# Background transfers of a two-block attention kernel sent one by one from a list, and its output operands added later

## The chip, the cores and the metric

The kernel runs on one core of a Trainium2 chip. The metric is the device time of one execution in microseconds; before the change the median of 3 runs is 2736.03 us (2734.36 to 2736.89).

## The reference

Two attention blocks work on the same input x (2048 tokens x 512) with weights of their own, and a gate mixes their outputs. All is float32; each block has 32 heads of 16 elements.

```python
def block(x, wqkv, wo):
    q, k, v = split_heads(x @ wqkv)              # 32 heads, each 2048 x 16
    p = softmax(einsum("bhqd,bhkd->bhqk", q, k) * 16 ** -0.5, axis=-1)
    return merge_heads(einsum("bhqk,bhkd->bhqd", p, v)) @ wo

g = sigmoid((x * gate_w).sum(-1, keepdims=True))
out = g * block(x, A_wqkv, A_wo) + (1 - g) * block(x, B_wqkv, B_wo)
```

## The kernel before, in words

The two blocks make 64 heads, in 8 groups (G = 0 to 7) of 8; groups 0 to 3 are block A. A head takes 16 *rounds*, so there are 1024. The main loop (lines 889 to 927) does four rounds in one *pass*: it runs through the string FULL letter by letter, and each letter puts one piece of work into the engines' queues, in an order that was written by hand.

- `e` computes a bank of scores (PE, L257) and its exponential (ACT, L259); a pass has 16 of them. The stationary rows of a head are its *stacks* k_st, q_st and x_st, read from DRAM by `load_stacks` (12 DMAs on SP, one head after next). Two more rows of q_st hold minus the row maximum, so that the exponent is already safe.
- `m`, `D` and `A` compute these maxima 14 rounds ahead, from a second set of scores (PE L188; DVE L194 and L206; ACT L201). Half a head's maxima at a time, every 8 rounds, are split into two float16 parts on GpSimd (`max_split`, L217 to L220, buffer mrow), transposed on DVE, and sent by SP to a DRAM buffer md and from there into q_st (`max_rows`, L227 and L230). The next scores of that half need them about one pass later.
- digits multiply p by v on PE (L835, operand vg, loaded by GpSimd in `load_v`). Every 8 rounds the accumulator goes out through ev to DRAM (od, L859), numerators and denominators together.
- `W` advances the *stream* `hidden()` by one step: the projections q, k and v of later heads (L276, L298), and at last the output projection (L576). `E` evicts a finished bank of it. What `W` finds not ready stays empty.

The stream has two phases. In the first it needs weights: w (one for each of q and k of a group, 512 KB, `load_w`) and w_big (for v, then wo of either block, 2 MB, `load_rows`). In the second, after group 7's projections, it needs each group's attention output: `prepare` sets a job for one of 14 pairs (G, i): `load_num` (8 DMAs of 128 KB: ot and o_part from od), `load_rb` (4 DMAs of 128 KB, the inverted denominators rb), then on GpSimd `add_num` (12 rounds after the loads) and `normalize` (3 rounds later). `later` holds such calls by round, and `due` runs them in the middle of a pass or at its start. The denominators come in with `load_den`, and are added and inverted by `add_den` (GpSimd) and `queue_inverse` (DVE).

Almost all DMAs are issued on the SP queue, in program order. SP waits at each one whose data another engine has still to write (od waits for ev, md for DVE, rd and the parts of q and k for DVE and GpSimd), and all DMAs behind it wait too; one that needs nothing is issued as soon as SP reaches it. The DMAs of SP use eight completion semaphores in turn, so at most eight are in flight. GpSimd executes in order as well.

Before the loop `first_projections` makes q and k of group 0 (eight banks split into `early`, three buffers), v of group 0 follows in half banks (`store_half_v`, to vd), the first half of head 0's maxima is computed beside them (`run_ahead`), and vg is loaded.

Of the kernel before, what the change touches and what calls it, by code (L numbers as in the profile page):

```python
# [33 lines left out]
P = 128  # L34
# [20 lines left out]
def gated_mha(ctx: ExitStack, tc: tile.TileContext, xT, x, wqkv_a, wo_a, wqkv_b, wo_b, gate_w, out):  # L55
# [42 lines left out]

    wqk = {}

    def load_w(queue, G, isk, k=0, n=None):
# [4 lines left out]
        load_rows(queue, wqk[G, isk], wqkv[s][:, o:o + P], k, n or KH)  # L106

    for k in range(0, KH, 2):
# [30 lines left out]

    def load_stacks(h, queue=nc.sync):  # L140
        dma, dma_q = nc.sync.dma_start, queue.dma_start
        s, hh = divmod(h, H)
        g, j = divmod(hh, HG)
        q, k = q_st[h % 3], k_st[h % 3]
        qs, ks, xs = qd[s][g], kd[s][g], xd[s][g]

        def pairs(t, step, n=S):
            v = t[0, j]
            return bass.AP(tensor=v.tensor, offset=v.offset, ap=[[n, DH], [step, 2], [1, n]])

        for b in HALVES:
            dma(k[b:b + 32], pairs(ks, HG * DH * S))
            dma_q(q[b:b + 32], pairs(qs, 0))
            dma(k[b + 32:b + 48], ks[0, j])
            dma_q(q[b + 32:b + 48], qs[1, j])
        x = x_st[h % 2]
        for b in HALVES:
            dma(x[b:b + 32], pairs(xs, HG * DH * 512, 512))
            dma(x[b + 32:b + SC], xs[0, j])

# [202 lines left out]
    def first_projections():  # L363
        early, rise = {}, xs.tile([P, 512], F32, name="rise_k")

        def split(isk, i, side, ps):
            t = early[isk, i, side] = xs.tile([P, 2, 512], F16, name="early", bufs=3)
            act.activation(t[:, 0], ps, AF.Copy, scale=UNIT)
# [26 lines left out]
    first_projections()  # L395
    load_stacks(0, nc.scalar)
    new_maxima(0)
# [144 lines left out]
    def load_num(G, i):  # L542
        k = SLOTS[G, i]
        part = nums["p", G, i] = T["late"].tile([P, 2, 512], F32, name="o_part", bufs=2)
        o = od[G]
        for p in range(2):
            for f, b in enumerate((64, 0)):
                for hh in range(2):
                    nc.sync.dma_start(
                        T["o"][b:b + 64, k + hh] if p == 0 else part[b:b + 64, hh],  # L550
                        bass.AP(tensor=o.tensor,
                                offset=o.offset + ((4 * hh * 2 + i) * 4 + 2 * p + f) * 32 * 512,
                                ap=[[2 * NQ * 32 * 512, 4], [512, DH], [1, 512]]))
# [5 lines left out]
    def load_rb(G, i):  # L559
        rb = nums["r", G, i] = T["late"].tile([P, 2, 512], F32, name="rb", bufs=2)  # L560
        r = rd[G]
        for f, b in enumerate((64, 0)):
            for hh in range(2):
                nc.sync.dma_start(rb[b:b + 64, hh],
                                  bass.AP(tensor=r.tensor, offset=r.offset + 4 * hh * S + i * 1024 + f * 512,
                                          ap=[[S, 4], [0, DH], [1, 512]]))

# [96 lines left out]
    for G in range(LAST):  # L664
        end = (G + 1) * HG * NT
        at(end + 4, load_den, G)
        at(end + 7, add_den, G)
        for i in range(4):
            at(end + 8 + 2 * i, queue_inverse, G, i)
    end = LAST * HG * NT  # L670
    for i in range(2):
        at(end + 6 + 4 * i, load_num, 6, i)
        at(end + 18 + 4 * i, add_num, 6, i)
        at(end + 23 + 4 * i, load_rb, 6, i)
        at(end + 32 + 4 * i, normalize, 6, i)
    now = [0]

    def until(r):
# [34 lines left out]
    def soon():  # L713
        return now[0] // 4 * 4 + 8

    def hidden():
# [12 lines left out]
        def qk(G):  # L729
            for isk in (1, 0):  # L730
                if isk:
                    load_w(nc.sync, G, 0)
                elif G < LAST:
                    load_w(nc.sync, G + 1, 1)
                for low in (0, 64):
# [4 lines left out]
        for G in range(1, NG):  # L740
            yield from qk(G)
            if G == 1:
                for n in range(8):
# [24 lines left out]

        r = soon()
        for G in range(4):  # L770
            ready = prepare(G, 0, r + 8 * G)
        for G in range(2):
            prepare(G, 1, r + 32 + 8 * G)
        yield from until(ready)
        yield from outs(range(4), 0, first)
        r = soon()
        for G in (2, 3):
            ready = prepare(G, 1, r + 8 * (G - 2))
        for G in (4, 5):
            done_b = prepare(G, 1, r + 16 + 8 * (G - 4))  # L780
        yield from until(ready - 5)
        yield from outs(range(4), 1, first)
        for b in HALVES:
            nc.sync.dma_start(w_big[b:b + 64, :6], wo[1][:384].rearrange("(k p) c -> p k c", p=64))
        nc.sync.dma_start(w_big[:DH, 6], wo[1][DM - DH:, :])
        nc.sync.dma_start(w_big[DH:, 6], wo[1][DM - P:DM - DH, :])
        r = soon()
        for G in (4, 5):
            prepare(G, 0, r + 8 * (G - 4))
        yield from until(max(done_b, r + 4))  # L790
        yield from outs((4, 5), 1, more)
        yield from until(LAST * HG * NT + 36)
        yield from outs((4, 5, 6), 0, more)
        yield from outs((6,), 1, more)

    stream = hidden()

# [91 lines left out]
    while r < ROUNDS:  # L889
# [9 lines left out]
        for code in order:  # L899
            if code == "e":  # L900
                if scored == 8:
                    due(r + 2)
                    if (r + 2) % NT == 4 and r // NT + 2 < NH:
                        load_stacks(r // NT + 2)
                score(2 * r + scored // 2, scored % 2)
                scored += 1
            elif code in "mDA":
                step(code)
            elif code == "E":
                empty()  # L910
            elif code == "W":
                now[0] = r + scored // 4
                next(stream, None)
# [48 lines left out]
```

## Time and profile before

| | |
|---|---|
| median of 3 runs | 2736.03 us |
| the profiled execution | 2732.4 us |
| its span | 2730.5 us |
| PE busy | 2543.5 us, 93% |
| ACT busy | 2401.1 us, 88% |
| DVE busy | 2375.3 us, 87% |
| GpSimd (POOL) busy | 410.2 us, 15% |
| PE's mean granted clock | 0.977 |
| moved by SP's queue (q1) | 172.81 MB, 22.5% of 16 DMA engines' time |

In the page's lines a digit is the busy share of a slice of 1/40 of the span, 68 us. In the view of waits a row reads: engine, what it was about to do, whose end it waited for, then the total in us, how often, and the longest. SPq is SP's queue, where only issuing takes time.

### The profile page before, as it was taken

Reading aid. Unit: us, or ns where it says so; the run is one execution under the profiler, and the core shown is the slowest. Engines: PE = TensorE matmul, PEld = TensorE weight load, DVE = VectorE, ACT = ScalarE, POOL = GpSimd, SP = SyncE. Lnnn points to the kernel's source line nnn. Section 1 sums busy time; section 2 is a strip of 40 time slices with the busy share of each in tenths; the row PEclk is TensorE's granted clock in tenths of the full one; section 3 lists DMA queues with packets and bytes.
Section 4 is the critical chain, followed back from the end, with each engine's and each line's share of the span. In section 5 each row is a group of like instructions: output and inputs, shape, how many; then the busy total and the mean of one; then the engine's idle time right before and its main releaser. Section 6 shows DMA issues by size and latency. Waiting matters only on the chain.

```text
span 2730.5 us, 169615 instructions
## 1 busy us (share of the span) xinstructions
PE 2543.5 (93%) x76566; PEld 1611.9 (59%) x76566; DVE 2375.3 (87%) x4604; ACT 2401.1 (88%) x4741; POOL 410.2 (15%) x809
## 2 busy tenths in 40 slices
PE   8899999999999999999999998689987998979987
PEld 4566665666666666666666665346644655545553
DVE  2889998999999999999999998679986988978884
ACT  1589998999999999999999998679986988978885
POOL 2133112111100001111111110121011001010003
PEclk9899999999999999999999999889998999989999
DMA  7422223232222212232222213222122122121103
GB/s 156 115 72 74 79 75 87 64 83 62 55 58 67 75 53 62 66 86 62 60 59 76 76 55 92 94 93 59 41 87 75 50 71 85 45 75 46 38 21 111
DMA packets 143790, 195.07 MB, mean 71 GB/s; under 512 B 38600, under 2 KB 88728, under 8 KB 143064
## 3 DMA queue, kind: packets, MB, share of 16 engines
q1 hardware_dynamic: 137528, 172.81, 22.5%
q8 instruction: 599, 9.81, 1.5%
q0 software_dynamic: 2560, 8.91, 1.3%
q10 hardware_dynamic: 2976, 2.49, 0.4%
q14 instruction: 127, 1.04, 0.1%
HBM read 117.56 MB, written 66.58 MB: 67 GB/s over the span
## 4 chain that ended last, share of the span: by engine, by line
PE 71%; DVE 10%; DMA 8%; POOL 3%; ACT 3%; issue 3%; SPq 1%; ACTq 0%; POOLq 0%; DVEq 0%
PE acc L835 33%; PE ps_m L188 13%; PE ps_st L257 12%; DVE mxp L194 6%; PE ps_p L276 5%; DMA md<-mt 4%; PE ps_st L188 3%; PE ps_p L576 2%; ACT p L259 2%; DVE ev L858 1%; PE ps_p L298 1%; DVE rise L206 1%; DMA o_part<-od 1%; ACT ev L858 1%; POOL stage L725 1%
## 5 line engine op out<-in xcount | busy, mean ns | idle before, releaser
L259 ACT ACTIVATE p<-ps_st 128x512 f32<-128x512 f32 x4068 | 2122.3, 640 | 190.3 <-PE ps_st L257 140.2
L835 PE MATMUL acc<-p,vg 64*17 64x384 f32 (+1 forms) x34784 | 2207.9, 368 | 22.9 <-issue 6.5
L194 DVE TENSOR_REDUCE mxp<-ps_m 128x1 f32<-128x512 f32 x3072 | 1944.8, 682 | 184.8 <-PE ps_m L188 152.7
L257 PE MATMUL ps_st<-q_st,k_st 50*32 50x512 f16 x16272 | 1568.7, 384 | 95.3 <-DMA q_st<-md 83.9
L188 PE MATMUL ps_m<-k_st,q_st 48*32 48x512 f16 x14336 | 1393.1, 381 | 24.0 <-DVE mxp L194 19.8
L835 PEld LDWEIGHTS acc<-p,vg 64*17 64x17 f32 x34784 | 982.3, 94 | 252.1 <-issue 27.8
L257 PEld LDWEIGHTS <-k_st 50*32 50x32 f16 x16384 | 665.8, 91 | 462.6 <-issue 202.4
L188 PEld LDWEIGHTS <-q_st 48*32 48x32 f16 x16384 | 549.7, 91 | 269.7 <-issue 178.2
L276 PE MATMUL ps_p<-x_sb,w 64*32 64x512 f32 x3648 | 480.9, 593 | 2.3 <-issue 2.3
L206 DVE CUSTOM_DVE_ANT_0 rise<-ps_m,rise 128x512 f32<-128x512 f32 x512 | 349.6, 683 | 69.5 <-PE ps_st L257 54.0
L201 ACT ACTIVATE rise<-ps_st 128x512 f32<-128x512 f32 x512 | 314.9, 615 | 60.7 <-PE ps_st L188 52.9
L576 PE MATMUL ps_p<-w_big,ot 64*32 64x512 f32 x1792 | 236.9, 593 | 27.0 <-DVE o_acc L767 25.1
L188 PE MATMUL ps_st<-x_st,q_st 48*32 48x512 f16 x2048 | 225.5, 380 | 0.2 <-ACT v_st L341 0.2
L218 POOL TENSOR_SCALAR mrow<-mrow 128x8 f32<-128x8 f32 x128 | 29.6, 232 | 1209.0 <-DVE mrow L217 1208.4
L322 POOL CAST parts<-stage 128x512 f16<-128x512 f32 x56 | 34.1, 608 | 830.7 <-DVE stage L702 437.0
L276 PE MATMUL ps_p<-w_big,x_sb 64*32 64x512 f32 x1024 | 134.6, 590 | 0.0
L276 PEld LDWEIGHTS ps_p<-x_sb,w 64*32 64x32 f32 x3648 | 117.1, 107 | 17.9 <-issue 4.1
L298 PE MATMUL ps_p<-w_big,x_sb 64*32 64x256 f32 x1280 | 87.5, 377 | 0.6 <-issue 0.6
L576 PEld LDWEIGHTS ps_p<-w_big,ot 64*32 64x32 f32 x1792 | 56.0, 107 | 46.6 <-DVE o_acc L767 28.0
L323 POOL TENSOR_TENSOR parts<-stage,parts 128x512 f16<-128x512 f32 x56 | 65.2, 1164 | 4.6
L298 PEld LDWEIGHTS ps_p<-w_big,x_sb 64*32 64x32 f32 x1280 | 43.6, 106 | 14.2 <-issue 2.8
L858 DVE COPY ev<-acc 128x512 f32<-128x512 f32 x64 | 44.1, 690 | 0.5 <-PE ps_m L188 0.2
(107 smaller groups left out, 766.7 us busy)
## 6 DMA issues: line engine op xcount, KB each, us to landing
od<-ev SPq DMA_DIRECT2D x126, 256.0 KB
k_st<-kd SPq DMA_DIRECT2D x128, 128.0 KB
q_st<-qd SPq DMA_DIRECT2D x126, 128.0 KB
vd<-v_st SPq DMA_DIRECT2D x64, 136.0 KB
vg<-vd POOLq DMA_DIRECT2D x32, 272.0 KB, 3.7
k_st<-kd SPq DMA_DIRECT2D x128, 64.0 KB
q_st<-qd SPq DMA_DIRECT2D x126, 64.0 KB
kd<-parts SPq DMA_DIRECT2D x56, 128.0 KB
```

The costliest lines, as they stand in the source:

```text
L188: pe.matmul(ps[j:j + 32], q[b:b + SC, t * P + j:t * P + j + 32], k[b:b + SC], start=True, stop=True, tile_position=(b, j))
L194: dve.tensor_reduce(o[:, c:c + 1], ps, op=ALU.max, axis=AX.X)
L201: act.activation(rises[m], ps, AF.Relu)
L206: dve.tensor_tensor_reduce(out=rise, in0=ps, in1=rise, scale=1.0, scalar=LOWEST, op0=ALU.add, op1=ALU.max, accum_out=o[:, 0:1])
L257: pe.matmul(ps[j:j + 32], k[b:b + SC + 2, kk * P + j:kk * P + j + 32], qv(b), start=True, stop=True, tile_position=(b, j))
L259: act.activation(pt[u][:, c * 512:(c + 1) * 512], ps, AF.Exp, scale=SCALE / UNIT ** 2)
L276: pe.matmul(ps[j:j + 32], a, m, start=k == 0, stop=k == last, tile_position=(b, j))
L298: pe.matmul(ps[j:j + 32, e * 256:(e + 1) * 256], x_sb[b:b + 64, i, k, o:o + 32], w_big[b:b + 64, k, g * P:(g + 2) * P], start=k == e == 0, ...
L323: pool.tensor_tensor(t[:n, 1], v[:n], t[:n, 0], op=ALU.subtract)
L576: pe.matmul(ps[j:j + 32], T["o"][b:b + 64, k, o + j % 64:o + j % 64 + 32], w_big[b:b + 64, g], start=first, stop=last, tile_position=(b, j))
L835: pe.matmul(acc[d:d + 17, qa * P:qb * P], v[b:b + 64, 2 * (w % n) + c if h == NH - 1 else w % n, j], pt[u][b:b + 64, c * 512 + qa * P:c * ...
L858: (dve.tensor_copy if w < NT or h == NH - 2 else act.copy)(ev, acc)
```

## The change

There is a list `waiting` of single DMAs. `drip(n)` issues the first n of it. In the main loop it is called with 1 after every second score bank, so two DMAs go out in a round. Into the list go: the stacks (at the front, `waiting[0:0] = ops`), w in four DMAs of 128 KB instead of two of 256 KB, w_big in 16 of 128 KB instead of two of 1 MB (for block A's second half of v, eight of 128 KB), and the output operands, whose 12 DMAs of a job were single ones before. A `mark` in the list notes the round in which everything ahead of it is out.

The jobs are now set by a second stream, `prepared()`, advanced once in a round: it puts a job's loads into the list, waits for their mark, and sets `add_num` 6 rounds later and `normalize` 8 rounds later. `hidden()` waits for the round in which its operands are ready. `load_den` goes from round 4 to round 8 after a group's end, `add_den` from 7 to 13, the inversions from 8, 10, 12, 14 to 14 to 17. Before the loop `early` has five buffers instead of three, the first `max_rows` and the stacks of head 1 come two to four steps earlier (the stacks one by one), and the four loads of the first vg stand behind all of v instead of two and two between.

The core of the diff:

```diff
+    def drip(n):
+        for _ in range(n):
+            if waiting:
+                fn, *a = waiting.pop(0)
+                fn(*a)
...
+    def drip_rows(t, src, n, last=KH):
+        waiting.extend((part_rows, t, src, b, k, n) for k in range(0, last, n) for b in HALVES)
...
+        if slow:
+            waiting[0:0] = ops
...
-            t = early[isk, i, side] = xs.tile([P, 2, 512], F16, name="early", bufs=3)
+            t = early[isk, i, side] = xs.tile([P, 2, 512], F16, name="early", bufs=5)
...
-                elif gone == n_ahead // 2 + 3:
+                elif gone == n_ahead // 2 + 1:
                     max_rows(0, 0)
-                elif gone == n_ahead // 2 + 6:
+                elif gone == n_ahead // 2 + 2:
+                    drip_w(1, 1)
                     load_stacks(1)
-                    load_w(nc.sync, 1, 1)
+                elif gone > n_ahead // 2 + 3 and gone % 2:
+                    drip(1)
...
-        if t in (2, 6):
-            for c in (0, 2) if t == 2 else (1, 3):
-                load_v(0, c)
...
-    load_wv(0, 2, 2)
+    for c in (0, 1, 2, 3):
+        load_v(0, c)
+    drip_rows(w_big[:, :, 256:], wqkv[0][:, 2 * DM + 256:], 2)
+    waiting.append((mark, "v"))
...
-        at(end + 4, load_den, G)
-        at(end + 7, add_den, G)
+        at(end + 8, load_den, G)
+        at(end + 13, add_den, G)
...
-    def prepare(G, i, r):
-        r = max(r, (G + 1) * HG * NT + 22)
-        at(r, load_num, G, i)
-        at(r + 3, load_rb, G, i)
-        at(r + 12, add_num, G, i)
-        at(r + 15, normalize, G, i)
-        return r + 18
...
+    def prepared():
+        added = []
...
+            for G, i in jobs:
+                yield from until((G + 1) * HG * NT + 26)
+                while len(added) > 1 and now[0] < added[-2] + 3:
+                    yield
+                waiting.extend((fn,) for fn in (*load_num(G, i), *load_rb(G, i)))
+                waiting.append((mark, ("in", G, i)))
+                yield from wait(("in", G, i))
+                r = now[0] + 6
+                at(r, add_num, G, i)
+                at(r + 2, normalize, G, i)
+                added.append(r)
+                flags["ready", G, i] = r + 5
...
-                load_wv(1, 0, NG)
+                drip_rows(w_big, wqkv[1][:, 2 * DM:], 1)
...
-        load_rows(nc.sync, w_big, wo[0], 0, KH)
+        drip_rows(w_big, wo[0], 1)
...
+                if scored % 4 == 0:
+                    now[0] = r + scored // 4
+                    next(prep, None)
                 score(2 * r + scored // 2, scored % 2)
                 scored += 1
+                if scored % 2:
+                    drip(1)
```

Three places of the program show how the SP queue is changed. The first is the start of the second phase, on SP, around the maxima md_115 of head 41. Before (a row is a line of the kernel, the operation, out<-in, the shape, and how often in a row):

```order
L549 DMA ot<-od_105 64x1x512 x4
L549 DMA o_part<-od_105 64x1x512 x4
L859 DMA od_110<-ev 128x512
L564 DMA rb<-rd_116 64x1x512 x4
L227 DMA md_115<-mt 4x32x32
L230 DMA q_st_219<-md_115 2x1024 x2
L524 DMA rd_120<-rn 16x4x128 x2
L549 DMA ot<-od_106 64x1x512 x4
L549 DMA o_part<-od_106 64x1x512 x4
L859 DMA od_110<-ev 128x512
L564 DMA rb<-rd_117 64x1x512 x4
L227 DMA md_115<-mt 4x32x32
```

And after the change at the same place:

```order
L899 DMA od_110<-ev 128x512
L589 DMA ot<-od_105 64x1x512 x4
L262 DMA md_115<-mt 4x32x32
L265 DMA q_st_219<-md_115 2x1024 x2
L589 DMA o_part<-od_105 64x1x512 x4
L601 DMA rb<-rd_116 64x1x512 x4
L589 DMA ot<-od_106 64x1x512 x2
L899 DMA od_110<-ev 128x512
L561 DMA rd_120<-rn 16x4x128 x2
L589 DMA ot<-od_106 64x1x512 x2
L589 DMA o_part<-od_106 64x1x512 x2
L262 DMA md_115<-mt 4x32x32
```

Before each md stood twelve loads and an od; now four loads stand between the od (or rd) and md, and the rest of the job stands behind md.

The second place is on SP where block A's v is done and w_big is loaded with block B's weights, around md_115 of head 8. Before:

```order
L345 DMA vd_103<-v_st_230 64x2x272 x2
L97 DMA w_big<-in_wqkv_b 64x8x512 x2
L97 DMA w_11575<-in_wqkv_a 64x8x128 x2
L227 DMA md_115<-mt 4x32x32
L230 DMA q_st_219<-md_115 2x1024 x2
```

After, with the stacks of the next head (k_st_216 and the rows up to x_st_223) in front of what is left of the list:

```order
L380 DMA vd_103<-v_st_230 64x2x272 x2
L116 DMA w_big<-in_wqkv_b 64x512 x3
L262 DMA md_115<-mt 4x32x32
L265 DMA q_st_219<-md_115 2x1024 x2
L106 DMA k_st_216<-kd_88 32x1x2048
```

Ahead of md there were 2.5 MB; now there are three portions of 128 KB, and the other 13 of w_big follow 8 to 12 rounds later.

The third place is on SP before the loop, where the last rows of group 0's v go to vd. Before, the stacks of head 1 (12 DMAs, the last two shown) and w stood ahead of them:

```order
L158 DMA x_st_224<-xd_95 32x1x512
L159 DMA x_st_224<-xd_95 16x512
L97 DMA w_1324<-in_wqkv_a 64x8x128 x2
L345 DMA vd_103<-v_st_229 64x2x272 x2
L345 DMA vd_103<-v_st_230 64x2x272 x2
L97 DMA w_big<-in_wqkv_a 64x8x256 x2
L97 DMA w_1620<-in_wqkv_a 64x8x128 x2
```

After:

```order
L265 DMA q_st_211<-md_113 2x1024 x2
L106 DMA k_st_216<-kd_87 32x1x2048
L106 DMA q_st_215<-qd_79 32x1x2048
L106 DMA k_st_216<-kd_87 16x2048
L380 DMA vd_103<-v_st_229 64x2x272 x2
L380 DMA vd_103<-v_st_230 64x2x272 x2
L106 DMA q_st_215<-qd_79 16x2048
```

Three stack loads are left ahead of the vd stores; the rest of the stacks, w and w_big stand behind them.

More of the change, by code (lines that the diff above doesn't have):

```diff
@@ L99, in gated_mha @@
     wqk = {}
+    waiting = []
+    def drip(n):
[3 more added lines that the diff above has]
+                fn(*a)
     def load_w(queue, G, isk, k=0, n=None):
@@ L106, in load_w, with part_rows, drip_w, begin @@
         load_rows(queue, wqk[G, isk], wqkv[s][:, o:o + P], k, n or KH)
+    def part_rows(t, src, b, k, n):
+        nc.sync.dma_start(t[b:b + 64, k:k + n], src[k * 64:(k + n) * 64].rearrange("(k p) c -> p k c", p=64))
+    def drip_w(G, isk):
+        s, g = divmod(G, NG)
+        def begin():
+            wqk[G, isk] = xs.tile([P, KH, P], F32, name=f"w{isk}")
+        def one(b, k):
+            if (b, k) == (0, 0):
+                begin()
+            o = isk * DM + g * P
+            part_rows(wqk[G, isk], wqkv[s][:, o:o + P], b, k, 4)
+        waiting.extend((one, b, k) for b in HALVES for k in (0, 4))
+    def drip_rows(t, src, n, last=KH):
+        waiting.extend((part_rows, t, src, b, k, n) for k in range(0, last, n) for b in HALVES)
+    def mark(name):
+        flags[name] = now[0]
+    flags, now = {}, [0]
     for k in range(0, KH, 2):
@@ L138, in gated_mha, with load_stacks @@
         x_st.append(const.tile([P, 512], F16, name=f"x_st{i}"))
-    def load_stacks(h, queue=nc.sync):
+    def load_stacks(h, queue=nc.sync, slow=True):
         dma, dma_q = nc.sync.dma_start, queue.dma_start
@@ L149, in pairs @@
             return bass.AP(tensor=v.tensor, offset=v.offset, ap=[[n, DH], [step, 2], [1, n]])
+        x = x_st[h % 2]
+        ops = []
         for b in HALVES:
[L152 to L156, printed above, removed]
-        for b in HALVES:
-            dma(x[b:b + 32], pairs(xs, HG * DH * 512, 512))
-            dma(x[b + 32:b + SC], xs[0, j])
+            ops += [(dma, k[b:b + 32], pairs(ks, HG * DH * S)), (dma_q, q[b:b + 32], pairs(qs, 0)),
+                    (dma, k[b + 32:b + 48], ks[0, j]), (dma_q, q[b + 32:b + 48], qs[1, j])]
+        for b in HALVES:
+            ops += [(dma, x[b:b + 32], pairs(xs, HG * DH * 512, 512)), (dma, x[b + 32:b + SC], xs[0, j])]
+        if slow:
+            waiting[0:0] = ops
+        else:
+            for fn, *a in ops:
+                fn(*a)
     LOWEST = -3.4028234e38
@@ L395, in gated_mha @@
     first_projections()
-    load_stacks(0, nc.scalar)
+    load_stacks(0, nc.scalar, slow=False)
     new_maxima(0)
@@ L543, in load_num @@
         k = SLOTS[G, i]
-        part = nums["p", G, i] = T["late"].tile([P, 2, 512], F32, name="o_part", bufs=2)
         o = od[G]
@@ L548, in load_num, with one, load_rb @@
                 for hh in range(2):
[L549 to L553, printed above, removed]
+                    def one(p=p, f=f, b=b, hh=hh):
+                        if (p, f, hh) == (0, 0, 0):
+                            nums["p", G, i] = T["late"].tile([P, 2, 512], F32, name="o_part", bufs=2)
+                            nums["r", G, i] = T["late"].tile([P, 2, 512], F32, name="rb", bufs=2)
+                        nc.sync.dma_start(
+                            nums["p", G, i][b:b + 64, hh] if p else T["o"][b:b + 64, k + hh],
+                            bass.AP(tensor=o.tensor,
+                                    offset=o.offset + ((4 * hh * 2 + i) * 4 + 2 * p + f) * 32 * 512,
+                                    ap=[[2 * NQ * 32 * 512, 4], [512, DH], [1, 512]]))
+                    yield one
+    def load_rb(G, i):
+        r = rd[G]
+        for f, b in enumerate((64, 0)):
+            for hh in range(2):
+                def one(f=f, b=b, hh=hh):
+                    nc.sync.dma_start(nums["r", G, i][b:b + 64, hh],
+                                      bass.AP(tensor=r.tensor, offset=r.offset + 4 * hh * S + i * 1024 + f * 512,
+                                              ap=[[S, 4], [0, DH], [1, 512]]))
+                yield one
     def add_num(G, i):
@@ L557, in add_num @@
         pool.tensor_tensor(v, v, nums.pop(("p", G, i)), op=ALU.add)
[L559 to L566, printed above, removed]
     def normalize(G, i):
@@ L665, in gated_mha @@
         end = (G + 1) * HG * NT
-        at(end + 4, load_den, G)
-        at(end + 7, add_den, G)
+        at(end + 8, load_den, G)
+        at(end + 13, add_den, G)
         for i in range(4):
[L669 to L676, printed above, removed]
+            at(end + 14 + i, queue_inverse, G, i)
     def until(r):
@@ L703, in copier, with wait @@
             else dve.tensor_copy
-    def prepare(G, i, r):
-        r = max(r, (G + 1) * HG * NT + 22)
-        at(r, load_num, G, i)
-        at(r + 3, load_rb, G, i)
-        at(r + 12, add_num, G, i)
-        at(r + 15, normalize, G, i)
-        return r + 18
-    def soon():
-        return now[0] // 4 * 4 + 8
+    def wait(*names):
+        while any(n not in flags or flags[n] > now[0] for n in names):
+            yield
+    def prepared():
+        added = []
+        for name, jobs in (("phase", ((0, 0), (1, 0), (2, 0), (3, 0), (0, 1), (1, 1))),
+                           (("out", 0, 0), ((2, 1), (3, 1), (4, 1), (5, 1))),
+                           (("out", 0, 1), ((4, 0), (5, 0), (6, 0), (6, 1)))):
+            yield from wait(name)
+            for G, i in jobs:
+                yield from until((G + 1) * HG * NT + 26)
+                while len(added) > 1 and now[0] < added[-2] + 3:
+                    yield
+                waiting.extend((fn,) for fn in (*load_num(G, i), *load_rb(G, i)))
[6 more added lines that the diff above has]
+                flags["ready", G, i] = r + 5
     def hidden():
@@ L731, in qk @@
                 if isk:
-                    load_w(nc.sync, G, 0)
+                    drip_w(G, 0)
                 elif G < LAST:
-                    load_w(nc.sync, G + 1, 1)
+                    drip_w(G + 1, 1)
                 for low in (0, 64):
@@ L742, in hidden @@
             if G == 1:
+                yield from wait("v")
                 for n in range(8):
@@ L753, in hidden @@
         second_phase()
-        load_rows(nc.sync, w_big, wo[0], 0, KH)
+        flags["phase"] = now[0] + 2
         def outs(groups, i, evict):
@@ L767, in more @@
             dve.scalar_tensor_tensor(o, ps, gate[1][:, t:t + 1], o, op0=ALU.mult, op1=ALU.add)
[L769 to L774, printed above, removed]
-        yield from outs(range(4), 0, first)
[L776 to L781, printed above, removed]
-        yield from outs(range(4), 1, first)
[L783 to L790, printed above, removed]
+        yield from wait(*(("ready", G, 0) for G in range(4)))
+        yield from outs(range(4), 0, first)
+        flags["out", 0, 0] = now[0]
+        yield from wait(*(("ready", G, 1) for G in range(4)))
+        yield from outs(range(4), 1, first)
+        flags["out", 0, 1] = now[0]
+        drip_rows(w_big, wo[1], 1, 6)
+        waiting.append((nc.sync.dma_start, w_big[:DH, 6], wo[1][DM - DH:, :]))
+        waiting.append((nc.sync.dma_start, w_big[DH:, 6], wo[1][DM - P:DM - DH, :]))
+        waiting.append((mark, "wo"))
+        yield from wait("wo")
+        yield from until(now[0] + 4)
+        yield from wait(("ready", 4, 1), ("ready", 5, 1))
         yield from outs((4, 5), 1, more)
-        yield from until(LAST * HG * NT + 36)
+        yield from wait(*(("ready", G, 0) for G in (4, 5, 6)))
         yield from outs((4, 5, 6), 0, more)
+        yield from wait(("ready", 6, 1))
         yield from outs((6,), 1, more)
-    stream = hidden()
+    stream, prep = hidden(), prepared()
     end = ROUNDS - NT
@@ L911, in gated_mha @@
             elif code == "W":
-                now[0] = r + scored // 4
                 next(stream, None)
```

## The prediction

> **What bounds the kernel now.** The page first: how long, which engine, and where the busy digits dip.
>
> ```profile
> span 2730.5 us, 169615 instructions
> PE 2543.5 (93%) x76566; PEld 1611.9 (59%) x76566; DVE 2375.3 (87%) x4604; ACT 2401.1 (88%) x4741; POOL 410.2 (15%) x809
> PE   8899999999999999999999998689987998979987
> PEclk9899999999999999999999999889998999989999
> ```
>
> PE (TensorE) is at nine tenths nearly everywhere and dips at the start and in slices 25 to 37, so the 187 us in which it is idle lie in a few places. The view of waits names them; first PE's own, then two of ACT and POOL that matter at the start.
>
> ```profile
> PE ps_st L257 <- DMA q_st<-md: 83.9, 13, 14.0
> PE ps_p L576 <- DVE o_acc L767: 25.1, 21, 1.8
> PE ps_m L188 <- DVE mxp L194: 19.8, 26, 2.8
> PE ps_st L257 <- issue: 9.3, 2, 5.0
> PE acc L835 <- DMA vg<-vd: 5.9, 1, 5.9
> ACT early L368 <- DMA qd<-early: 10.6, 2, 6.7
> POOL vg L269 <- DMA vd<-v_st: 39.6, 2, 20.5
> ```
>
> One wait leads: 13 times PE stands before the score product of L257 because the row maxima of the head have not come back from DRAM (`max_rows`: mt to md, md to q_st). The first row below, from the page's list of DMAs, counts 128 such trips; only 13 made PE wait. What stands ahead of a late one on the SP queue is in the timeline of SP; the last three rows are a trip with nothing ahead of it.
>
> ```profile
> md<-mt SPq DMA_DIRECT2D x128, 8.0 KB
> ...
> 1715.95 2.27 SPq L549 DMA_DIRECT2D ot<-od  x4
> 1718.58 2.37 SPq L549 DMA_DIRECT2D o_part<-od  x4
> 1721.81 0.36 SPq L859 DMA_DIRECT2D od<-ev  x1
> 1722.22 3.55 SPq L564 DMA_DIRECT2D rb<-rd  x4
> 1726.81 0.54 SPq L227 DMA_DIRECT2D md<-mt  x1
> 1735.40 0.55 SPq L230 DMA_DIRECT2D q_st<-md  x2
> ...
> 1881.02 0.34 SPq L859 DMA_DIRECT2D od<-ev  x1
> 1886.14 0.58 SPq L227 DMA_DIRECT2D md<-mt  x1
> 1888.12 0.52 SPq L230 DMA_DIRECT2D q_st<-md  x2
> ```
>
> Alone, md is back after 1.98 us (1886.14 to 1888.12). Behind twelve operand loads it takes 8.6 us (1726.81 to 1735.40), though it moves only 8 KB. Two stretches show what the DMA engines do meanwhile (columns: busy of PE, PEld, DVE, ACT, POOL, then clock, DMA share, GB/s):
>
> ```profile
> 1727.00:1735.00 8.00, 8.00 (x244) 4.19 (x228) 7.81 (x16) 8.00 (x18) 2.02 (x1) 1.00 0.27 97
> 1672.00:1680.00 8.00, 6.37 (x182) 3.33 (x171) 7.26 (x14) 6.92 (x15) 0.00 (x0) 1.00 1.08 205
> ```
>
> While md hangs behind operand loads, a share of 0.27 of 16 engines is busy, so about four of them, at 97 GB/s: those loads run on a quarter of the engines, and md sits in the same quarter. A portion of 128 KB takes 131,072 / 97,000 = 1.35 us there. While w_big streams (second row), all engines are full at 205 GB/s, and PE is down to 6.37 of 8 us.
>
> Now what the dips cost. One pass of the hand-written order (4 rounds) has 16 score banks and so 16 ACTIVATEs of L259; counting these per stretch gives the pace and the excess (columns: us, ACT busy, clock, DMA share, GB/s).
>
> ```profile
> 600.00:1040.00 440.00, 383.84 (x739) 1.00 0.23 63
> 2341.00:2395.00 54.00, 49.93 (x96) 1.00 0.19 57
> 97.00:116.00 19.00, 8.34 (x16) 0.78 0.81 172
> 426.00:453.00 27.00, 17.50 (x33) 0.87 0.70 152
> 1675.00:1834.00 159.00, 100.31 (x193) 0.86 0.31 98
> 2003.00:2041.00 38.00, 25.45 (x50) 0.91 0.25 87
> 2041.00:2120.00 79.00, 50.81 (x97) 0.89 0.22 72
> 2216.00:2250.00 34.00, 25.24 (x49) 0.90 0.36 82
> 2395.00:2457.00 62.00, 41.87 (x80) 0.89 0.21 70
> ```
>
> Undisturbed the pace is 440 / 739 = 0.595 us a bank where a W step (a projection piece from the stream) fills in, 9.53 us a pass, and 54 / 96 = 0.5625 us, 9.00 us a pass, without W steps. The excess of the seven disturbed stretches: 19 - 16 x 0.595 = 9.5; 27 - 33 x 0.595 = 7.4; 159 - 193 x 0.5625 = 50.4; 38 - 50 x 0.5625 = 9.9; 79 - 97 x 0.595 = 21.3; 34 - 49 x 0.5625 = 6.4; 62 - 80 x 0.5625 = 17.0. The last six make 112.4 us. That is more than the 83.9 us of named waits because each wait also leaves a lower clock (0.86 to 0.91) and because the stretches with w_big (426, 1675, 2216) hold PE waits put down to "issue" instead.
>
> **The change part by part.** *Operand loads in portions.* In the second phase 14 jobs of twelve DMAs (ot, o_part, rb) stood in bursts of eight and four. Now they go out one at a time, two in a round, and the burst ahead of md is four portions at most. But SP is not paced by rounds: it runs ahead to its next gate (od, md or rd, which wait for another engine), so four portions between an od and the md behind it go out at once, about half a pass, 5 us, before md. Four take 4 x 1.35 = 5.4 us, so md meets an almost empty queue. Where portions before the od are still unfinished too, md meets up to four: I count six such trips in the new order. What a late trip costs is bounded by the pair above: 8.6 us instead of 1.98 is 6.6 us late, and PE waited
>
> ```profile
> 1737.12 0.40 PE L257 MATMUL ps_st<-q_st,k_st 50*32 50x512 f16 x4 [1.89 <-DMA q_st<-md]
> ```
>
> 1.89 us, so 4.7 us are covered by the distance between the trip and its first use. Four portions (5.4 us) cost up to 0.7 us, and with SP itself late or the clock lowered about 2: six times 2 is 12 us that stay. Bounds: 0, and 31 (14 jobs of 6 rounds each lie across 14 x 6 / 8 = 10.5 half-heads, each at 3 us).
>
> *w_big and w in portions.* 2 x 1 MB become 16 x 128 KB. With at most a few in flight md waits for about 0.65 us of each (131,072 / 205,000), within the cover, and PE's "issue" waits of 4 to 5 us, which stand only where the engines are full, should go. Their excess is in the six stretches. The number of DMAs on SP rises by 72 in all (40 of w_big and w become 112); at 2.27 / 4 = 0.57 us each that is 41 us of SP time, under SP's own waiting:
>
> ```profile
> SPq L859 <- ACT ev L858: 627.8, 61, 15.9
> ```
>
> SP stands 627.8 us for this one gate alone, so these 41 us cost nothing; without that cover they would cost 41. The Trainium skill, DMA: Bandwidth & Descriptors, section Bandwidth, speaks against this part: batch DMAs to 1 MiB or more. Its section Anatomy of one DMA fits 2.0 us fixed plus bytes / 436,000 per DMA (on GpSimd's path); an estimate by that page is 72 x 2.0 = 144 us more, if nothing overlapped. The rows disagree for this kernel: four loads are issued in 2.27 us, so fixed parts overlap; by the page alone the sum would be 2768.
>
> *GpSimd six rounds behind.* add_num followed its loads by 12 rounds after the first, and normalize 12 after rb; now add_num stands 6 rounds after the last portion. POOL executes in order, and behind a waiting add_num stands the maxima's split (L218), whose md the scores need. Six rounds are 6 x 2.25 = 13.5 us, more than the eight portions that SP can have in flight (10.8 us), so POOL should not wait; what it waited before is inside the six stretches. Until data is ready the stream yields nothing and W steps stay empty; the pieces are only moved, and passes without them run at 9.00 instead of 9.53, so it costs nothing as long as the stream ends before the last head, which it does by its rounds, three passes later than before.
>
> *Start.* `early` has five buffers instead of three, and the vg loads stand behind one another after the vd stores, no longer behind a burst of stacks and weights.
>
> ```profile
> 33.05 3.55 DMA qd<-early
> 38.66 2.40 DMA qd<-early
> 95.53 2.91 DMA vd<-v_st
> 99.02 9.27 DMA vg<-vd
> ...
> 93.57 2.57 SPq L345 DMA_DIRECT2D vd<-v_st  x4
> ```
>
> The first two lie on the chain that ended last and are waits for a buffer (5.95 us); two more buffers remove about 5, and POOL's rise step is next. The last vd stores were issued at 93.57, behind 14 loads; three loads now stand ahead of them, so they go some 6 us earlier, vg (9.27 us among w_big and w) lands in about 4, and PE's 5.9 us wait goes; late next is nothing that the trace shows. I take 5 + 6 = 11 us; bounds 4 (only part of the buffers' wait) and 15.5 (5.95 + 9.5, the whole excess of the first stretch).
>
> *Stacks from the list.* Twelve DMAs over six rounds, from the front of the list, are needed eight rounds (19 us) after the last: covered.
>
> *Sum.* The profiled execution took 2732.4 us (span 2730.5 and 1.9 around it); the median of the runs is 2736.0, 3.6 above. 2732.4 - 112.4 - 11 + 12 = 2621.0; with 3.6, 2624.6.
>
> **The rivals.** *Half of it stays.* Two portions a round ask 2.70 us of the quarter's time in a round of 2.25 to 2.38 us: the portions alone overfill four engines while a job lasts, and jobs follow each other. For: 0.27 and 97 GB/s look like a ceiling. Against: a job is only six rounds, so the surplus is 12 x 1.35 - 6 x 2.25 = 2.7 us. If md meets a full ring of eight portions (10.8 us, 6.1 beyond the cover) in all 10.5 half-heads, 64 us stay instead of 12: 2677.
>
> *The portions bunch.* Nothing on SP paces a portion, so all of a job could still go out behind one gate, ahead of md. Then the four operand stretches keep their excess (about 50.4 - 6 for w_big, 9.9, 21.3, 17.0, together 92.6) and only w_big and the start gain, 7.4 + 6.4 + 6 + 11 = 31: 2705. Against it: in the new order md stands between the portions of a job, not after all of them.
>
> *Slower: a portion has its own price.* If the 72 added DMAs, each with the trip of the smallest one, 1.98 us, came onto the path (SP late for od, md and the parts), 143 us would come back: 2768. It decides at 111 / 72 = 1.5 us an added DMA; below that the change stays faster. For: SP issues in order and everything passes it. Against: SP's 627.8 us of waiting. The page's rule on batching above is this rival.
>
> **How the numbers follow.** Forecast 0.80; half stays 0.11; bunched 0.05; own price 0.04. The predicted time is the forecast's, 2625. Its own bounds: 112.4 + 15.5 - 0 gives 2608, 112.4 + 4 - 31 gives 2651. For what an excess counted in whole passes can be off, and to take in the near side of the first rival, the range is 2604 to 2658. A measurement of this kernel can tell about 0.2%, 5.5 us, from no change. Faster 0.95, same 0.02, slower 0.03: the first three cases are faster and the fourth slower, and 0.01 of the third and of the fourth is put to no change.
>
> **What would show it.** Right: PE's wait for q_st<-md falls from 83.9 to under 20 us, no "issue" wait over 2 us at w_big, no vg wait; the stretches of the second phase run at 9.0 to 9.5 us a pass; md trips between 2 and 7 us. Wrong: md trips of 8 us and more still there (first two rivals); SP's wait at L859's place near zero and score banks late everywhere (third); or the start unchanged.

## The result and the profile after

The changed kernel takes 2628.06 us (median of 4 runs, 2624.47 to 2629.69) against 2736.46 us for the kernel before, measured beside it (2734.36 to 2738.33): ratio 0.9602, 95% interval 0.9586 to 0.9619. The predicted 2625.0 is 3.1 us off; the profiled execution took 2624.47, where the sum said 2621.0. The page of after:

```profile
span 2622.6 us, 169689 instructions
PE 2529.7 (96%) x76566; PEld 1608.1 (61%) x76566; DVE 2369.7 (90%) x4604; ACT 2397.6 (91%) x4741; POOL 411.5 (16%) x809
PE   8999999999999999999999999989999999899997
PEclk9899999999999999999999999999999999999999
```

The dips of PE in slices 25 to 37 are nearly gone, and with them the low clock there. The view of waits of after (PE's own, and SP's longest):

```profile
SPq L899 <- ACT ev L898: 573.1, 60, 12.8
PE ps_st L292 <- DMA q_st<-md: 21.7, 7, 6.5
PE ps_m L223 <- DVE mxp L229: 20.5, 33, 2.8
PE ps_p L618 <- DVE o_acc L815: 12.2, 7, 1.8
PE ps_st L292 <- issue: 0.9, 2, 0.7
```

The wait for md fell from 83.9 to 21.7 us, vg's wait is gone, and the "issue" waits at w_big with it. SP still stands 573.1 us at the od gate: 55 less than before. That fits added DMAs that came out of SP's waiting, but doesn't prove it, since the whole run is shorter too. Its timeline shows the new order at work at the first md of the second phase, and further down where it fails; the last row is from DVE and ends with mt, the data that this md sends:

```profile
1668.64 0.37 SPq L899 DMA_DIRECT2D od<-ev  x1
1669.10 2.30 SPq L589 DMA_DIRECT2D ot<-od  x4
1672.70 0.54 SPq L262 DMA_DIRECT2D md<-mt  x1
1677.30 0.53 SPq L265 DMA_DIRECT2D q_st<-md  x2
...
1723.78 3.79 SPq L589 DMA_DIRECT2D o_part<-od  x4
1728.23 0.55 SPq L899 DMA_DIRECT2D od<-ev  x1
1730.05 4.48 SPq L601 DMA_DIRECT2D rb<-rd  x4
1735.26 0.54 SPq L262 DMA_DIRECT2D md<-mt  x1
1744.13 0.53 SPq L265 DMA_DIRECT2D q_st<-md  x2
...
1730.82 0.20 DVE L259 STREAM_TRANSPOSE mt<-mparts 128x32 f16<-128x32 f16 x1
```

Behind four portions md is back after 4.60 us (1672.70 to 1677.30), inside the cover. In the second place eight went out in 10.8 us around an od, and md took 8.87 us. SP was late as well: mt was done at 1731.02, and SP issued md at 1735.26, 4.24 us later, since it stood in the rb loads until then. Both together, 4.24 + 8.87 - 1.98 = 11.1 us, less the 4.7 us of cover, make the 6.5 us wait. Three more trips took 8.8 to 11.1 us: those issued at 1812.63, 2046.84 and 2368.56.

Where the 107.9 us of span went, by stage. The times are starts of passes, a pass counted as 16 of the ACTIVATEs of the exponential. The load of wo into w_big, at 1669 us before the change and so in the row from 642 to 690, comes at 1036 to 1069 us after it, in the row above; in us:

| stage | before | after |
|---|---|---|
| start to round 10 | 125.8 | 122.7 |
| rounds 10 to 130 | 300.5 | 297.9 |
| 130 to 146 (w_big of block B) | 45.4 | 38.1 |
| 146 to 642 | 1194.8 | 1191.4 |
| 642 to 690 (w_big, first jobs) | 157.7 | 120.9 |
| 690 to 1014 | 851.7 | 796.5 |
| 1014 to the end | 54.6 | 55.1 |

One thing in the last but one row the prediction did not see. The eight-piece output stage of groups 0 to 3, i = 0, takes 16 passes. In the windows that hold just these passes (columns: us; busy and number of the exponential's ACTIVATEs; clock, DMA share, GB/s) it ran 152.9 us before:

```profile
1824.20:1977.10 152.90, 133.04 (x257) 1.00 0.19 55
```

and 163.0 after:

```profile
1797.90:1960.90 163.00, 133.69 (x257) 1.00 0.20 61
2228.60:2318.50 89.90, 66.52 (x128) 1.00 0.22 71
```

The second row is the four-piece stage, 8 passes at 11.24 us instead of 9.5. The clock is 1.00 there, and only the four-piece stage has named waits of more than 0.3 us (ps_p for o_acc, 7 of about 1.7 us). The string FULL says which slot is at fault there: it has four W a pass, and an E (eviction) behind the second, third and fourth, but none between the first and the second. A bank of four or eight pieces ends on the same slot each time; here that is the first W, so the next bank's first piece, at the second W, finds ps_p full. This stage lay so before the change too, with the same 7 waits.

The eight-piece stages are another case. By the order of PE's instructions they start on the fourth W and end on the third, with an E behind it; before, the first of them started on the first W. Their passes that no md disturbs take 10.0 us instead of 9.5, with no wait over 0.3 us, and no run here shows why. The rest of the 10 us stands in the passes around the md trips at 1812.63 and 1835.47. On which slot a stage starts depends on when its operands were ready, so moving the operands moved that.

### The profile page after: what moved, and what is told of

Same layout as the page of the kernel before. It is cut to its first block, busy times and chain, and to the rows that moved or that the text cites. A ratio compares the mean times of both kernels' runs of the same rounds, so it can differ in the third digit from the quotient of the medians.

```text
span 2622.6 us, 169689 instructions
## 1 busy us (share of the span) xinstructions
PE 2529.7 (96%) x76566; PEld 1608.1 (61%) x76566; DVE 2369.7 (90%) x4604; ACT 2397.6 (91%) x4741; POOL 411.5 (16%) x809
## 4 chain that ended last, share of the span: by engine, by line
PE 75%; DVE 11%; DMA 4%; POOL 3%; ACT 3%; issue 2%; SPq 1%; ACTq 0%; POOLq 0%; DVEq 0%
PE acc L875 35%; PE ps_m L223 14%; PE ps_st L292 12%; DVE mxp L229 7%; PE ps_p L311 6%; PE ps_st L223 3%; PE ps_p L618 2%; DMA md<-mt 2%; ACT p L294 2%; PE ps_p L333 1%; DVE ev L898 1%; DVE rise L241 1%; ACT ev L898 1%; POOL stage L771 1%; DMA w<-in_wqkv_a 1%
## 5 line engine op out<-in xcount | busy, mean ns | idle before, releaser
L292 PE MATMUL ps_st<-q_st,k_st 50*32 50x512 f16 x16272 | 1559.2, 382 | 24.1 <-DMA q_st<-md 21.7
L253 POOL TENSOR_SCALAR mrow<-mrow 128x8 f32<-128x8 f32 x128 | 29.8, 233 | 1233.5 <-DVE mrow L252 1233.1
L333 PEld LDWEIGHTS ps_p<-w_big,x_sb 64*32 64x32 f32 x1280 | 44.1, 107 | 12.8 <-issue 1.0
## 6 DMA issues: line engine op xcount, KB each, us to landing
k_st<-kd SPq DMA_DIRECT2D x128, 128.0 KB
q_st<-qd SPq DMA_DIRECT2D x126, 128.0 KB
kd<-parts SPq DMA_DIRECT2D x56, 128.0 KB
```

The costliest lines, as they stand in the source:

```text
L292: pe.matmul(ps[j:j + 32], k[b:b + SC + 2, kk * P + j:kk * P + j + 32], qv(b), start=True, stop=True, tile_position=(b, j))
L333: pe.matmul(ps[j:j + 32, e * 256:(e + 1) * 256], x_sb[b:b + 64, i, k, o:o + 32], w_big[b:b + 64, k, g * P:(g + 2) * P], start=k == e == 0, ...
```

## Experiments

All times are medians; ratios are against the kernel before, measured beside each group of runs (2737.56, 2738.08 and 2736.20 us). Where two changed kernels are compared, the difference of their medians and that of their ratios agree within 3 us, and both are uncertain by about 0.003 (8 us).

**The list undone for the jobs: all twelve loads at once.**

```diff
-                waiting.extend((fn,) for fn in (*load_num(G, i), *load_rb(G, i)))
-                waiting.append((mark, ("in", G, i)))
+                for fn in (*load_num(G, i), *load_rb(G, i)):
+                    fn()
+                mark(("in", G, i))
```

> The changed kernel, but each job's twelve operand loads are issued together in the round in which the job is set, not two in a round; weights and stacks stay in portions and add_num stays six rounds behind. Theory of the portions (md was late because 128 KB loads stood ahead of it on the same four DMA engines): the operand stretches get back what they lost, 92.6 - 18 = about 75 us, so 2695 to 2710, with PE's wait for q_st<-md at 70 us or more. Rival, GpSimd (the gain came from the additions and denominators that were moved back, so that GpSimd no longer blocks the split of the maxima): no more than 10 us come back, 2628 to 2640.

Measured 2766.85, ratio 1.0106 (1.0074 to 1.0139): 139 us more than the changed kernel, far over either forecast. PE's waits, and SP and POOL at the first jobs:

```profile
PE ps_st L292 <- DMA q_st<-md: 87.3, 8, 24.1
PE ps_m L223 <- DVE mxp L229: 78.8, 34, 21.7
```

```profile
1658.32 2.32 SPq L589 DMA_DIRECT2D ot<-od  x4
...
1678.18 4.69 SPq L601 DMA_DIRECT2D rb<-rd  x4
...
1688.84 2.34 POOL L608 TENSOR_TENSOR ot<-ot,o_part 128x1024 f32<-128x1024 f32 x1 [14.72 <-DMA k_st<-kd]
1691.15 0.23 POOL L253 TENSOR_SCALAR mrow<-mrow 128x8 f32<-128x8 f32 x1
```

Two jobs went out back to back (24 loads, 1658.3 to 1682.9), and the mark, now set at issue, no longer says that data is near. add_num (L608) stood on GpSimd until 1688.84, and the maxima's split (L253) behind it until 1691.15. So both theories hold, and my form of the experiment switched on the second with the first: the wait on mxp is GpSimd's share.

**w_big whole again**, and **w_big in 16 portions issued one after another** (for block B's v likewise):

```diff
-        drip_rows(w_big, wo[0], 1)
+        load_rows(nc.sync, w_big, wo[0], 0, KH)
```

```diff
-        drip_rows(w_big, wo[0], 1)
+        for k in range(KH):
+            for b in HALVES:
+                part_rows(w_big, wo[0], b, k, 1)
```

> The changed kernel, but w_big for block B's v and for block A's output comes in two DMAs of 1 MB again (at the place where its portions now enter the list). Theory of the portions: the stalls of 7.4 and about 6 us come back, so about 2641, with waits of 4 to 5 us of PE put down to issue, or late md trips. Rival (the place in the order made the stall, not the size): within 3 us of 2628.

> As the run with w_big whole, but as 16 DMAs of 128 KB issued one right after the other. Theory: SP needs 0.57 us to issue one and the engines 0.65 us to move it, so the portions hardly queue up and size alone is enough: 2628 to 2633. Rival (only the spacing over rounds helps): as with w_big whole, about 2641.

Measured 2643.48 (0.9651, 0.9626 to 0.9677) and 2648.32 (0.9674, 0.9653 to 0.9695): 13 and 20 us above the change. The second of the two loads is that of wo, which the change also moved; both runs load it at the changed place. PE's waits of the two, whole first:

```profile
PE ps_st L292 <- DMA q_st<-md: 18.3, 6, 4.6
PE acc L875 <- issue: 7.3, 4, 5.9
PE ps_st L292 <- issue: 6.0, 5, 4.2
```

```profile
PE ps_st L292 <- DMA q_st<-md: 35.5, 8, 7.6
PE acc L879 <- issue: 3.8, 6, 1.4
```

The first was forecast. The second was not: small portions end the "issue" waits, but sent one behind another they put md late instead (7.6 us). Size alone gains nothing; what gains is the gap between portions. The Trainium skill, DMA: Bandwidth & Descriptors, section Bandwidth, advises batches of 1 MiB or more; by the first run two batches of 1 MB cost 13 us here against 16 spaced portions. They cost it in the "issue" waits (13.3 us in its last two rows, 2.4 us in the same rows after the change); the wait for md is no longer than after the change (18.3 against 21.7 us).

**GpSimd two rounds behind the mark instead of six** (`r = now[0] + 2`).

> The changed kernel, but add_num stands 2 rounds behind its last portion instead of 6 (and normalize 4 instead of 8). Theory of the portions: GpSimd waits some us for loads still in flight, mostly where nothing urgent stands behind it: 2625 to 2638. Rival, GpSimd (the six rounds carry the gain): 2660 or more.

Measured 2640.12 (0.9636, 0.9610 to 0.9663), 9 us above the change by the ratios, near the edge of what they tell apart; it lies just beyond the forecast and far from the rival's 2660. The trace shows the path: POOL waits for rb 38.9 us in 8 times (after: 5.2 in 4), and PE for md 37.5 us in 11 times. The four-piece stage also starts on another slot in this run, at about 10.8 instead of 11.5 us a bank, which hides some 5 us. So six rounds are worth about 10 to 15 us.

**The kernel before, with its operand loads spread.** Same order, same bursts of operand loads, same bytes; the order of the dimensions in the loads' addresses is swapped (of ot and o_part here, of rb likewise). The run also brings wo's rows of w_big in 16 and 12 DMAs of 128 KB, issued one after another, instead of two of 1 MB and two of 768 KB:

```diff
-                                ap=[[2 * NQ * 32 * 512, 4], [512, DH], [1, 512]]))
+                                ap=[[512, DH], [2 * NQ * 32 * 512, 4], [1, 512]]))
```

> The kernel before with its order untouched, bursts of twelve and all; only the operand loads ot, o_part and rb (and wo's rows in w_big, 128 KB each) have the 16 blocks' dimension of 16 in place of 4 as their outermost, so that each is spread over all engines and not over about four. Quarter theory (md is late because the loads ahead of it in the burst share four engines, 1.35 us each): at 205 GB/s a load takes 0.65 us, eight in flight 5.2 us, md comes 3.5 us late instead of 6.6, which is under the cover of 4.7; the operand stretches' excess of 92.6 us goes nearly all, w_big's and the start's stays: 2645 to 2670, PE's wait for q_st<-md under 25 us. Rival (what costs is that SP issues twelve loads ahead of md, or the completion of eight in flight, whatever engines they use): 2725 to 2740, the wait stays near 84 us.

Measured 2657.36 (0.9704, 0.9687 to 0.9721): the quarter theory's number; the rival is out. SP in the same burst, its stretch by the DMA share and GB/s with PE's wait behind it:

```profile
1694.56 3.49 SPq L553 DMA_DIRECT2D ot<-od  x4
1698.10 3.41 SPq L553 DMA_DIRECT2D o_part<-od  x4
1701.62 0.52 SPq L866 DMA_DIRECT2D od<-ev  x1
1702.18 3.00 SPq L568 DMA_DIRECT2D rb<-rd  x4
1705.28 0.58 SPq L231 DMA_DIRECT2D md<-mt  x1
1707.97 0.53 SPq L234 DMA_DIRECT2D q_st<-md  x2
```

```profile
1698.10:1705.30 7.20, 6.96 (x194) 3.12 (x179) 7.20 (x17) 7.14 (x16) 0.00 (x0) 1.00 0.61 176
...
PE ps_st L261 <- DMA q_st<-md: 22.2, 6, 6.3
```

Twelve loads ahead of md, as before, and md is back in 2.69 us instead of 8.6: the share is 0.61 instead of 0.27, and 176 GB/s instead of 97. The Trainium skill, DMA: Bandwidth & Descriptors, section Why a DMA increments its semaphore by 16 and not by 1, says that a DMA is spread over the largest number of engines, up to 16, that divides the slowest dimension of both its sides; with 4 and with 16 outermost the rows agree.

That the swap and not wo's portions gave the 81 us doesn't follow from this run alone. But w_big ran at a share of 1.08 before, so it needed no spreading (an outermost 4 was in the operand loads only), and here PE waits 6.35 us for the md behind its 16 portions, more than the 4.28 us of "issue" that it waited at that load before. And the two runs with all twelve loads at once, the one above and the one with spread loads below, have wo in the same portions and differ in the dimensions alone: 2767 and 2661 us. Four waits for md are left in the main loop, and they are SP's: there md is back in 2.2 to 2.7 us, but SP issues it 5.8 to 10.9 us after its data was ready. The run also bears on GpSimd's part in the change: POOL still stands 88.3 us for the denominators (dn; 92.6 before, 5.0 after the change), PE's wait for mxp is 19.5 us as before (19.8), and the gain came all the same.

**The changed kernel with spread loads**, and **with spread loads and bursts**:

> The changed kernel with operand loads and wo's rows spread over all 16 engines (outermost dimension 16 in place of 4); order and spacing as changed. Quarter theory: what is left of late md trips (PE's wait for q_st<-md 21.7 us, an excess of some 18 us) goes: 2608 to 2616, the wait under 6 us. Rival (the rest is SP's own lateness): 2624 to 2632, the wait stays near 20.

> The changed kernel with a job's twelve loads issued at once again (as in the run of that kind before, 2767), but over 16 engines. If the spacing matters only because four engines are slow, the access pattern alone does it: 2608 to 2625, PE's wait for q_st<-md under 10 us. If bursts are bad in themselves (eight loads in flight ahead of md, GpSimd's fixed six rounds): over 2680.

Measured 2608.02 (0.9524, 0.9508 to 0.9540): 20 us under the change. The only wait for md left is the tail's:

```profile
PE ps_m L227 <- DVE mxp L233: 20.5, 32, 2.8
PE ps_st L296 <- DMA q_st<-md: 4.7, 1, 4.7
```

With bursts on top, 2661.10 (0.9726, 0.9705 to 0.9747), between my two numbers. Its waits, PE's and GpSimd's:

```profile
PE ps_m L227 <- DVE mxp L233: 41.2, 32, 9.1
PE ps_st L296 <- DMA q_st<-md: 26.1, 6, 9.6
POOL ot L612 <- DMA rb<-rd: 72.7, 10, 16.1
```

So slow engines are the larger half of a burst's price (2767 to 2661), not all of it. The other half is SP itself: md is back in 2.0 to 2.5 us here, but where PE waits for it in the main loop SP had issued it 5 to 13 us after its data was ready. Against the spread kernel without bursts PE waits 21 us more for md and 21 more for mxp, the latter behind GpSimd, which stands 72.7 us for rb. Another 5 us are the slots: the later stages end on the first W again, and the wait for o_acc grows from 13.7 to 18.4 us.

**Four portions a round** (drip after every score bank, on four engines):

> The changed kernel with a portion after every score bank, four in a round, over four engines as changed. Quarter theory: four portions ask 5.4 us of the quarter in a round of 2.25 us, so a job's twelve queue up, and md behind them: the wait for q_st<-md grows from 21.7 to 50 us or more: 2650 to 2700. Rival (only what stands in one piece ahead of md on SP counts, which spacing of any kind breaks up): 2622 to 2635.

Measured 2721.88 (0.9947, 0.9926 to 0.9967), 94 us above the change: the theory's direction, past its range. Before one md now stand, around an od:

```profile
1685.62 4.00 SPq L589 DMA_DIRECT2D o_part<-od  x4
1689.67 1.61 SPq L601 DMA_DIRECT2D rb<-rd  x3
1691.38 0.40 SPq L899 DMA_DIRECT2D od<-ev  x1
1691.83 0.53 SPq L601 DMA_DIRECT2D rb<-rd  x1
1692.40 4.14 SPq L589 DMA_DIRECT2D ot<-od  x4
1697.82 0.54 SPq L262 DMA_DIRECT2D md<-mt  x1
1706.64 0.53 SPq L265 DMA_DIRECT2D q_st<-md  x2
```

The trip is 8.8 us again, and PE waits 96.5 us for md (13 times). With the list at this rate 15 us of the gain are left. This is the state of the rival in which portions bunch (it said 2705).

**Where an output stage starts.** In both kernels `bank` of a new output stage waits until the first W of a pass:

```diff
+            while slot[0]:
+                yield
...
+                slot[0] = order[:place].count("W")
```

> The kernel before, in which every stage of the output projection waits for the first W of a pass (slot A) before it starts; loads and waits as before. Alignment theory (a bank whose last piece falls on A is evicted only at the next W, and PE then stands 1.8 us before the next bank): the 4-piece stages gain 14 us, the 6-piece 9, the 2-piece 12, the eight-piece first stage loses nothing: 2695 to 2712, and the wait of ps_p for o_acc (25.1 us, 21 times) falls under 10. Rival (those 1.8 us are hidden elsewhere, and the excess of the second phase is md's alone): 2730 to 2745, since the stages are only started up to a pass later.

> The changed kernel, in which every stage of the output projection starts at slot A. Alignment theory: first eight-piece stages 152.8 us per 16 passes as before the change instead of 163.0 and 159.3, so -10 and -6.5; the two 4-piece stages 9.6 instead of 11.3 us a pass, -12; together 2595 to 2603. Rival (the slow passes of these stages come from the added loads that run beside them, not from where the stage starts): 2624 to 2632.

Measured 2710.67 (0.9904, 0.9881 to 0.9927) and 2610.79 (0.9532, 0.9514 to 0.9551): 27 and 17 us gained; the ps_p wait for o_acc is gone in both. The second is less than the forecast 29. The four-piece stage gave most of it (second row below: 78.3 us for 8 passes instead of 89.9); the first eight-piece stage gained only about 1, as the first row of the aligned kernel shows:

```profile
1796.80:1958.90 162.10, 134.42 (x256) 0.99 0.21 61
2233.10:2311.40 78.30, 67.15 (x129) 1.00 0.22 72
```

Its passes free of md run at 9.6 us instead of 10.0, but one stands 14.90 us, 3.0 above the same pass of the changed kernel: a late md took most of it back. I had also put all of the stage's 10 lost us to the slot, when some of them were md's. The kernel has one four-piece stage, where the forecast speaks of two.

**Both, spread and aligned:**

> The changed kernel with both: output stages that start at slot A, and operand loads and wo's rows over all 16 engines. If the two costs lie in different passes (md waits there, ps_p waits here), the gains add: 20 from the engines, 17 from the alignment and some 5 more that a longer md wait took back there: 2582 to 2594. If they are the same idle time seen twice: 2600 to 2610.

Measured 2584.14 (0.9442, 0.9423 to 0.9461): the gains add, 44 us under the change and the best version of this study. Its page has no dip left between start and end:

```profile
PE   8999999999999999999999999999999999999997
```

**Three early buffers:**

> The changed kernel with three early buffers again. The prediction took 5 us for the two more: 2630 to 2636. Rival (the scores start no earlier with five, 99.0 us after the start against 96.8 before, since the rise step on GpSimd sets that): 2624 to 2630, the ACT wait for early's DMA back.

Measured 2626.68 (0.9605, 0.9584 to 0.9626): no difference that can be told from the change (0.9602). In its profile the waits are back (ACT 12.8 us for early's DMA) and the scores start at 104.2 us instead of 99.0, but the median does not show these 5 us. The profiled execution is the slowest of the four (2632.84 us; the others took 2626.30 to 2626.91), so its later start may be its own. This stays open.

## Why the prediction was right, step by step

- *What bounds the kernel.* Shown: the loads on four engines ahead of md were the cost. Spreading them, with their order kept, takes 81 us off the kernel before.
- *What a late trip costs.* The prediction's pair (8.6 us, PE waits 1.89) bounds only trips that SP issues in time. The longer waits in the same row, up to 14.0 us, are those where SP was late as well. One of them:

```profile
1695.10 0.20 DVE L224 STREAM_TRANSPOSE mt<-mparts 128x32 f16<-128x32 f16 x1
1704.81 0.54 SPq L227 DMA_DIRECT2D md<-mt  x1
1714.08 0.52 SPq L230 DMA_DIRECT2D q_st<-md  x2
1715.72 0.62 PE L257 MATMUL ps_st<-q_st,k_st 50*32 50x512 f16 x4 [11.90 <-DMA q_st<-md]
```

  SP issued md 9.5 us after mt was done, and the trip took 9.27 us: 9.5 + 9.27 - 1.98 - 4.7 = 12.1, where PE waited 11.9. With SP's own lateness counted, the cover of 4.7 us fits this wait and the 6.5 us one after the change.
- *The six stretches, -112.4, less 12 that stay.* In the first phase w_big gave 45.4 - 38.1 = 7.3 for 7.4. In the second, 105.0 - 12 = 93 was forecast, and 36.8 + 55.2 - 0.5 = 91.5 came. The six late trips were counted rightly: outside the tail PE waits six times, 16.8 us in all, but at 2.8 us each instead of 2. The residue was undersized: spreading the loads shows that it is worth 20 us, inside the bounds of 0 and 31. The step that failed is "four portions at most": eight went out where SP ran on behind a late od, and four trips took 8.8 to 11.1 us. Another 6.0 of the 107.9 us came in rounds 10 to 130 and 146 to 642, where nothing was forecast; the other runs differ among themselves by as much there, so that part is luck.
- *W steps that only move cost nothing.* True in the sum alone. The prediction took every W pass at 9.53 us; a stage's pace depends on the slot in which it starts. The two eight-piece stages took 163.0 and 159.7 us, against 152.9 for the first before. By the passes that no md disturbs (10.0 us, against 9.5 and 9.7 before), some 13 us are the slots' price; this is an estimate. Between rounds 930 and 1014 the later stages won 15 us (218.5 to 203.5), as they no longer ended on the first W. That the two nearly cancel is luck. The price of ending there was in before already, in the row of ps_p for o_acc (25.1 us, 21 times) that the prediction showed and didn't use: 12.1 us of it lie in the four-piece stage and stay, 13.0 us in the later stages and went.
- *SP's 72 DMAs hidden.* Right as far as the runs show: its gate still has 573 us, and w_big in 16 pieces with gaps is 13 us faster than in two. That is against a price of their own, the slower rival.
- *GpSimd six rounds behind.* Right: it waits 5.2 us for rb, and with two rounds 38.9 (part of its price is hidden by the slots, as said).
- *Start, -11.* Oversized in the one pair of profiles (3.1 by round 10). That point varies: 125.8, 128.0 and 128.3 us in the three profiles with the old start, 118.2 to 122.8 in ten with the new one; the means differ by 6.5. The first loop pass gives 8 (19.4 to 20.7 us down to 11.2 to 12.6): vg was sized about right. The two buffers' 5 did not show in the times.
- *Rivals.* Half stays, and bunching, need more than four loads ahead of md; the run with four a round makes that state and its price.

The markers: no vg wait and no "issue" wait over 2 us, as said; md's wait 21.7 instead of under 20; four trips of 8.8 to 11.1 us and one of 7.0 outside 2 to 7, so that the first two rivals' sign, trips of 8 us and more, was there too (4 times, 13 before), without their price; and passes with W of 10 and 11.2 us outside 9.0 to 9.5.

## What to carry to other kernels

When a small urgent transfer is late, look at the DMA share of the stretch first: here a steady 0.27 meant that the loads ahead of it used a quarter of the engines. Swapping two dimensions is a small edit to try first: alone it came with 81 us where the change gave 108, and it gave 20 more on top of the change. Count the issuing queue's own lateness beside the trip. A background list needs a rate that the engines can take (two portions a round left six late trips, four a round lost all but 15 us of the gain), and a consumer on an in-order engine has to be set by the last portion, not by the first. In a hand-written order, a stage that moves by one slot may change its pace: price each stage by its own passes, not by a mean.

## What the runs showed of the hardware beside that

- TensorE has waits put down to "issue" of 3 to 6 us when w_big comes in pieces of 0.75 to 1 MB, and none over 2.0 us in the runs in which they come in 128 KB portions, even at once. The traces point at its instructions. A queue of kind "instruction" (q8) moves blocks of 16 KB, one every 4.1 us by the median. In all nine waits over 3 us (three in the kernel before, three in its aligned form, two with w_big whole, one in the kernel before with spread loads) such a block starts within the wait, 8.0 to 10.1 us after the last one, and PE goes on 1.4 to 1.7 us after it is through. No run changes that queue alone, so this is argued, not shown.
- The first weights make PE wait 5.0 to 7.2 us at the start of every run here, whatever the kernel; the change leaves that as it was.
